# SwiGLU after polysketch attention on one core: value products of three batches as three one-pass products

## The chip, the core and the metric

The kernel runs on one core of a Trainium2 chip. The metric is the device time of one execution in microseconds, the median over several runs. Engines are named as in the profile: PE is TensorE (matrix products), PEld its weight loads, DVE is VectorE, ACT is ScalarE, POOL is GpSimd, SP is the engine that issues most DMAs.

## What is computed

Two stages follow each other. The first is attention with a polynomial sketch: for every token x of q and k two small projections a = S1 x and b = S2 x are formed (8 numbers each), and their outer product is the feature vector phi(x) (64 numbers). Then

```
kv  = sum over s of phi(k_s) v_s^T          z = sum over s of phi(k_s)
out = (phi(q) kv) / (phi(q) z + 1e-6)
```

for 4 batches, 4 heads, 1088 tokens and 32 numbers per head. The heads side by side make a matrix x of 4352 tokens by 128. The second stage is a SwiGLU block with d_ff = 1536:

```
g   = x @ w_gate
val = x @ w_val
y   = (silu(g) * val) @ w_out
```

Inputs and the output are fp32 (the kernel also takes 64-bit floats and narrows them on the chip).

## The kernel before

**Tiles.** x is kept transposed in SBUF as `xT` (128 by 4352). The tokens of a batch are cut into three blocks of 384, 384 and 320, so there are 12 blocks. d_ff is cut into 12 chunks of 128. A `unit(i, j)` (L765) is block i and chunk j: one product with `wg` into a PSUM bank `g`, one with `wv` into a bank `u`, SiLU of g on ScalarE into `sg` (L779), and on VectorE the gate product sg * u into a slot of `hbuf` (L790). `down()` (L798) multiplies the slot by `wo` and accumulates a block's 12 chunks in the bank `acc`; after the last one, `store` (L829) turns the block on VectorE (L833) and sends it out. There are 144 units, each with three fp32 products.

**Order.** The schedule is written out by hand: each engine runs its instructions in the order in which the program emits them, and waits where an operand or a buffer is not there. In batch 0 the attention comes first, then units in a hand-made list `seq` (30 units, after six early ones), with the narrowing of the weights in between. From number z = 17 of that list on a down product follows each unit; when the list ends, the remaining down products of batch 0 are drained three at a time. Then comes a loop over batches 1 to 3 and z = 0 to 35 (L1034). Each turn emits one unit, the down product that is due (`LAG = 2`: two units stay open), and one piece of the attention of later batches.

**Attention in pieces.** `attentions()` (L532) is a generator. `parts_of(n)` advances it by n pieces, most of which are one VectorE instruction; in batch 1, at z = 0, 4, 6, 7 and 8, two pieces are emitted. `group()` runs it to the next place where small TensorE products are due. There are three such places: the head of the second block of batch 1 (z = 12), the head of batch 2, and the head of its third block. A group emits `numerators` (L720), which uses the double banks `a` and `b` and writes x of a later stretch into `xT`, then, but for the last one, `values` (L634), which needs the sums of key features, and at the first group the sketches of the next batch.

**Sums.** `feature_sums` (L490) adds the key features of a batch on GpSimd in four instructions (L494), the first over 1024 columns. `key_features` (L324) and L679 are VectorE products with both inputs in SBUF, L686 is a reduction and L710 a transpose.

**PSUM.** Eight banks are given out by name: `g0`, `g1`, `g2` and `acc` singly, `a` and `b` in pairs. Units take turns over the single ones: over all four in batch 0, and over `g0` to `g2` once down products use `acc`:

```python
    free_banks = ["g0", "g1", "g2", "acc"]
    turn = [0]

    def bank(tag=None):
        if tag is None:
            tag = free_banks[turn[0] % len(free_banks)]
            turn[0] += 1
        return psum.tile([P, TB], FP32, tag=tag, name="bank")
```

Of the kernel before, what the change touches and what calls it, by code (L numbers as in the profile page):

```python
# [6 lines left out]

FP32 = mybir.dt.float32
I32 = mybir.dt.int32
U32 = mybir.dt.uint32  # L10
I64 = mybir.dt.int64
# [7 lines left out]
def kernel(  # L19
# [64 lines left out]
    free_banks = ["g0", "g1", "g2", "acc"]  # L84
    turn = [0]

    def bank(tag=None):
        if tag is None:
            tag = free_banks[turn[0] % len(free_banks)]
            turn[0] += 1  # L90
        return psum.tile([P, TB], FP32, tag=tag, name="bank")

    def wide(tag):
        return psum.tile([P, 2, TB], FP32, tag=tag, name=tag)

    nc.scalar.preload_act_table(AF.Silu)

# [359 lines left out]
    def divide(b, x0, n, nd, among=()):  # L457
# [29 lines left out]
        for name in among[1:]:  # L487
            part(name, 0)

    def feature_sums(phk):  # L490

        rows = phk[:].rearrange("p c h i j -> p c (h i j)")
        s = apool.tile([P, 4, H * F], FP32, tag="zs", name="zs")
        add = lambda o, a, b: nc.gpsimd.tensor_tensor(out=o, in0=a, in1=b, op=ALU.add)  # L494
# [37 lines left out]
    def attentions():  # L532

        yield from turns(1)
        kp, qp = wide("a"), wide("b")
        for ps, products in ((kp, key_products), (qp, query_sketches)):
            for i, c in enumerate(kpieces):
                products(ps[:, i, :], *c)
        ka = apool.tile([P, NC * H, R], FP32, tag="kas", name="kas")
        qab = apool.tile([P, 2, NC * H, R], FP32, tag="qab", name="qab", bufs=2)
        fac = None, qab

        def sketch(ps, i):  # L550
            c0, c1 = kpieces[i]
            return ps[:, i, 0 : 64 * (c1 - c0)].rearrange("p (x t r) -> p x t r", t=2, r=R)

        for i, (c0, c1) in enumerate(kpieces):
            nc.scalar.copy(ka[:, H * c0 : H * c1, :], sketch(kp, i)[:, :, 0, :])
        phk = apool.tile([P, NC, H, R, R], FP32, tag="phk", name="phk")
        for n, (i, c0, c1) in enumerate(((0, 0, 3), (0, 3, 5), (1, 5, 7), (1, 7, 9))):
            first = H * (c0 - kpieces[i][0])
            kb = sketch(kp, i)[:, first : first + H * (c1 - c0), 1, :]
            key_features(phk, (ka[:, H * c0 : H * c1, :], kb), c0, c1)  # L560
            if n < 2:
                q0, q1 = kpieces[n]
                nc.scalar.copy(
                    qab[:, :, H * q0 : H * q1, :], sketch(qp, n).rearrange("p x t r -> p t x r")
                )
            if n % 3 != 1:
                yield
        zs = feature_sums(phk)
        for i, _ in enumerate(turns(2)):
            if i % 2:  # L570
                yield
        kvz = wide("a")
        values(kvz[:, 0, :], phk, zs)
        kq = wide("b")
        fac2, copies = sketches([
            (0, NC - 1, kq[:, 0], kq[:, 1]),
            (NC - 1, NC, kvz[:, 1, 0 : 2 * F], kvz[:, 1, 2 * F : 4 * F]),
        ])
        spread = spread_out(1, kvz[:, 0, :])
        for _ in range(4):  # L580
            yield
            run_copies(copies, 1)
        step = query_step(1, fac, spread)
# [10 lines left out]
        numerators(1, spread, 3, NC)  # L594
        kv = bank()
# [6 lines left out]
        run_copies(copies, 2)  # L602
        yield
# [158 lines left out]

    lates = []

    def unit(i, j, late=False, between=(None, None)):  # L765


        t0, n = blocks[i]
        g, u = bank(), bank()
        for o, w in ((g, wg), (u, wv)):  # L770
            if between[0] and w is wv:
                between[0]()
            nc.tensor.matmul(  # L773
                o[:, 0:n], w[:, j, :], xT[:, t0 : t0 + n], start=True, stop=True
            )
# [3 lines left out]
        nc.scalar.activation(sg[:, 0:n], g[:, 0:n], AF.Silu)  # L779
        slot_of[i, j] = slots.pop(0)  # L780
        hj = hbuf[:, slot_of[i, j], :]
        hidden[i, j] = hj
        todo.append((i, j))
        if late:
            if between[1]:
                between[1]()
            nc.scalar.copy(hj[:, 0:n], u[:, 0:n])
            lates.append((hj[:, 0:n], sg[:, 0:n]))
        else:
            nc.vector.tensor_tensor(  # L790
                out=hj[:, 0:n], in0=sg[:, 0:n], in1=u[:, 0:n], op=ALU.mult
            )
# [5 lines left out]
    def down():  # L798

        i, j = todo.pop(0)  # L800
        n = SPLIT if i == LAST else blocks[i][1]
        if j == 0:
            acc[i] = bank("g1" if i == 1 else "acc")
        nc.tensor.matmul(  # L804
            acc[i][:, 0:n],
            wo[:, j, :],
            hidden[i, j][:, 0:n],
            start=(j == 0),
            stop=(j == NCH - 1),
        )  # L810
        if i != LAST:
            hidden.pop((i, j))
            slots.append(slot_of[i, j])
        if j == NCH - 1:
            store(i, n)

    def straight(ps, j):

# [180 lines left out]
    seq += [(i, j) for i in (1, 2) for j in range(3, 6)]  # L999
    seq += [(i, j) for j0 in (6, 9) for i in range(3) for j in range(j0, j0 + 3)]  # L1000
    order = [(i, j) for i in range(3) for j in range(NCH)]
    for z, (i, j) in enumerate(seq):
        if z == 17:
            free_banks.pop()
            turn[0] %= 4
        unit(i, j)
        for p in parts.get(z, ()):
            part(*p)
        if z in (24, 25, 26):
            catch_up()  # L1010
        if z == 6:
            load_k(1)
            load_v(1, [nc.sync] * 4)
            load_q(1)
# [30 lines left out]
    for j in range(NCH):  # L1045
        if todo and j % 4 == 0:
# [40 lines left out]
```

## Time and profile before

| | |
|---|---|
| time, median of 3 (range) | 305.88 us (305.69 to 307.71) |
| span of the profiled execution | 304.3 us |
| TensorE busy, share of the span | 298.0 us, 98% |
| TensorE weight loads | 190.3 us, 63% |
| VectorE | 170.0 us, 56% |
| ScalarE | 93.8 us, 31% |
| GpSimd | 37.9 us, 12% |
| mean granted TensorE clock | 0.998 |

How to read it: a line of a profile names the engine, the line of the kernel, and what it writes and reads; `xN` is the number of records. Weight loads run beside products. Ends of matmuls are modelled, so the step from one start to the next tells more than a record's length. The batch-0 list with its down products runs until about 92.5 us, the loop over batches 1 to 3 from there to about 298 us. The three groups begin at 114.6, 163.1 and 212.2 us.

### The profile page before, as it was taken

The page shows a single profiled execution, that of the slowest core. Times are in us where ns is not written, and L with a number is a line of the kernel's source. Part 1 is how long each engine was busy: PE and PEld are TensorE (multiplying, and loading weights), DVE is VectorE, ACT ScalarE, POOL GpSimd, SP SyncE. Part 2 cuts the span into 40 slices and gives each one's busy share as a digit, 9 for nine tenths or more (in the row PEclk, how much of TensorE's full clock was granted, in tenths as well). Part 3 has the DMA queues.
Part 4 walks back from the last instruction along what each step waited for, and adds up shares of the span by engine and source line. Part 5 has one row for each costly group of instructions (what it writes and reads, how often), then busy time and mean ns, then how long its engine had stood idle before and what let it go on. Part 6 is the DMA issues. An engine that isn't in the chain of part 4 may idle for free.

```text
span 304.3 us, 5402 instructions
## 1 busy us (share of the span) xinstructions
PE 298.0 (98%) x2179; PEld 190.3 (63%) x2179; DVE 170.0 (56%) x334; ACT 93.8 (31%) x219; POOL 37.9 (12%) x54
## 2 busy tenths in 40 slices
PE   8899999999999999999999999999999999999995
PEld 7545566657565556556666655555676556676664
DVE  3997988692536991788932478822423322333321
ACT  3566764422102222322222222222322222222230
POOL 3216222174000050070000000000000000000000
PEclk9999999999999999999999999999999999999999
DMA  7563490404511000400100200100100100100101
GB/s 195 150 193 106 119 302 7 149 15 149 113 28 22 0 2 22 108 0 0 26 3 2 49 0 0 28 0 0 23 5 0 22 1 2 26 0 2 21 0 26
DMA packets 26136, 14.57 MB, mean 48 GB/s; under 512 B 18688, under 2 KB 24192, under 8 KB 26112
## 3 DMA queue, kind: packets, MB, share of 16 engines
q1 hardware_dynamic: 25456, 14.13, 18.5%
q8 instruction: 17, 0.28, 0.4%
q10 hardware_dynamic: 656, 0.10, 0.2%
q14 instruction: 7, 0.06, 0.1%
HBM read 11.41 MB, written 2.23 MB: 45 GB/s over the span
## 4 chain that ended last, share of the span: by engine, by line
PE 97%; DVE 1%; issue 0%; ACT 0%
PE bank L773 58%; PE bank L804 28%; PE bank L194 2%; PE a L730 1%; PE b L289 1%; PE bank L335 1%; PE a L819 1%; PE a L301 1%; PE bank L348 0%; PE bank L301 0%; PE a L392 0%; PE a L444 0%; PE a L335 0%; PE b L301 0%; PE b L730 0%
## 5 line engine op out<-in xcount | busy, mean ns | idle before, releaser
L790 DVE TENSOR_TENSOR hbuf<-sg,bank 128x384 f32<-128x384 f32 (+1 forms) x138 | 72.9, 529 | 99.5 <-PE bank L773 97.7
L779 ACT ACTIVATE sg<-bank 128x384 f32<-128x384 f32 (+1 forms) x144 | 68.0, 473 | 163.1 <-PE bank L773 159.9
L773 PE MATMUL bank<-xT,wg 128*128 128x384 f32 (+1 forms) x288 | 112.5, 472 | 0.0
L773 PE MATMUL bank<-xT,wv 128*128 128x384 f32 (+1 forms) x288 | 111.5, 469 | 0.2 <-DVE wv L239 0.2
L804 PE MATMUL bank<-hbuf,wo 128*128 128x384 f32 (+2 forms) x288 | 105.1, 460 | 0.0
L773 PEld LDWEIGHTS bank<-xT,wv 128*128 128x128 f32 x288 | 54.5, 190 | 33.7 <-DVE hbuf L790 0.9
L804 PEld LDWEIGHTS bank<-hbuf,wo 128*128 128x128 f32 x288 | 54.6, 190 | 32.0
L773 PEld LDWEIGHTS bank<-xT,wg 128*128 128x128 f32 x288 | 53.7, 190 | 32.2 <-issue 1.6
L494 POOL TENSOR_TENSOR zs<-hbuf 128x1024 f32<-128x1024 f32 x2 | 4.7, 2359 | 51.6 <-DVE hbuf L324 37.6
L833 DVE STREAM_TRANSPOSE o<-bank 128x384 f32<-128x384 f32 (+2 forms) x12 | 6.6, 549 | 7.8 <-PE bank L804 7.4
L679 DVE TENSOR_TENSOR phq<-spread,qab 128x768 f32<-128x768 f32 x9 | 9.7, 1075 | 0.5 <-DMA spread<-spread 0.5
L221 ACT ACTIVATE exp<-exp,rebias 128x384 int32<-128x384 int32 (+3 forms) x15 | 8.3, 551 | 2.4 <-DVE exp L216 1.7
L710 DVE STREAM_TRANSPOSE phT<-phq 128x768 f32<-128x768 f32 x9 | 8.7, 968 | 0.1
L686 DVE TENSOR_REDUCE dot<-phq 128x96 f32<-128x768 f32 x9 | 8.5, 947 | 0.1
L324 DVE TENSOR_TENSOR phq<-qab 128x768 f32<-128x768 f32 x9 | 8.5, 942 | 0.0
L747 ACT COPY xT<-a 128x64 f32<-128x64 f32 (+3 forms) x7 | 2.3, 367 | 18.2 <-PE b L730 11.8
L224 DVE SCALAR_TENSOR_TENSOR exp<-raw,exp 128x384 int32<-128x384 int32 (+2 forms) x14 | 7.0, 503 | 0.0
L230 DVE SCALAR_TENSOR_TENSOR man<-raw,man 128x384 f32<-128x384 uint32 (+2 forms) x14 | 6.9, 493 | 0.0
L222 ACT ACTIVATE man<-man 128x384 f32<-128x384 int32 (+3 forms) x15 | 6.8, 452 | 0.0
L494 POOL TENSOR_TENSOR zs<-zs 128x512 f32<-128x512 f32 (+1 forms) x6 | 6.6, 1101 | 0.5
L239 POOL TENSOR_TENSOR wg<-man,exp 128x384 f32<-128x384 f32 (+1 forms) x5 | 4.0, 805 | 18.2 <-DVE man L230 14.0
L274 DVE STREAM_TRANSPOSE kT<-kld 128x384 f32<-128x384 f32 (+2 forms) x9 | 5.9, 688 | 0.3 <-DMA kld<-in_k_dram 0.3
(127 smaller groups left out, 161.4 us busy)
## 6 DMA issues: line engine op xcount, KB each, us to landing
kld<-in_k_dram SPq DMA_DIRECT2D x4, 544.0 KB, 4.3
vld<-in_v_dram SPq DMA_DIRECT2D x12, 144.0 KB, 5.1
qld<-in_q_dram SPq DMA_DIRECT2D x3, 544.0 KB, 4.2
raw<-in_moe_w_out_dram SPq DMA_DIRECT2D x4, 384.0 KB, 4.9
out_dram<-o SPq DMA_DIRECT2D x28, 48.0 KB, 1.9
raw<-in_moe_w_gate_dram SPq DMA_DIRECT2D x3, 384.0 KB, 3.6
raw<-in_moe_w_val_dram SPq DMA_DIRECT2D x3, 384.0 KB, 3.3
out_dram<-o SPq DMA_DIRECT2D x16, 40.0 KB, 1.7
```

Of the source, the lines that this page charges most:

```text
L221: nc.scalar.activation(e[:], e[:], AF.Relu, bias=rebias[: shape[0], :], scale=8.0)
L224: nc.vector.scalar_tensor_tensor(out=e[:], in0=hi, scalar=-(1 << 31), in1=e[:], op0=ALU.bitwise_and, op1=ALU.bitwise_or,)
L230: nc.vector.scalar_tensor_tensor(out=f, in0=lo, scalar=2.0**-52, in1=f, op0=ALU.mult, op1=ALU.add)
L324: engine.tensor_tensor(out=phk[:, c0:c1, :, :, :].rearrange("p c h i j -> p (c h) i j"), in0=ka.unsqueeze(3).to_broadcast([P, n, R, R]), i ...
L494: add = lambda o, a, b: nc.gpsimd.tensor_tensor(out=o, in0=a, in1=b, op=ALU.add)
L679: nc.vector.tensor_tensor(out=phq[:, c0:c1, :, :, :], in0=zrep.unsqueeze(1).to_broadcast([P, n, H, R, R]), in1=f.unsqueeze(3).to_broadcast ...
L686: nc.vector.tensor_reduce(out=dot[:, x, :], in_=phq[:, c0:c1, :, :, :].rearrange("p c h j i -> p (c h) j i"), axis=AX.X, op=ALU.add,)
L710: nc.vector.transpose(out=phT[:, :, :, c0:c1, :].rearrange("p h g c t -> p c (h g) t"), in_=phq[:, c0:c1, :, :, :].rearrange("p c h (g i) ...
L773: nc.tensor.matmul(o[:, 0:n], w[:, j, :], xT[:, t0 : t0 + n], start=True, stop=True)
L779: nc.scalar.activation(sg[:, 0:n], g[:, 0:n], AF.Silu)
L790: nc.vector.tensor_tensor(out=hj[:, 0:n], in0=sg[:, 0:n], in1=u[:, 0:n], op=ALU.mult)
L804: nc.tensor.matmul(acc[i][:, 0:n], wo[:, j, :], hidden[i, j][:, 0:n], start=(j == 0), stop=(j == NCH - 1),)
```

## The change

The value products of batches 1 to 3 are computed otherwise. An fp32 number is cut into a high part of about 12 bits and the rest, each stored as float32r[...]. With w = w1 + w0 and x = x1 + x0, and B = 4096, the program forms

```
d = (w1 - B w0) @ (x1 - B x0)
p = w1 @ x1 + (B w0) @ x0
val = (1 + 1/B) p - d / B
```

which is Karatsuba's way to the four products of parts: three one-pass products in place of one fp32 product. The purpose is to give TensorE less work. The pieces are:

- `cut_weights(c)`: for each third of four chunks, high part on ScalarE, rest on GpSimd, B times the rest on ScalarE, difference on GpSimd; 16 instructions of 384 columns in all, from z = 23 to 29 of the batch-0 list.
- `cut_tokens(i)`: for a block, high part x1 on ScalarE, rest x0 on GpSimd, difference xd on VectorE; for most blocks it is emitted at chunk 6 of the block before.
- `cut_unit(i, j)`: three one-pass products into two banks `d` and `p`, the gate product as before into `g`; u = -d/B on ScalarE, (1 + 1/B) p + u on VectorE, and the gate product with SiLU on GpSimd. After `feature_sums` the next four cut units have their gate product on VectorE (`aside=False`), while GpSimd adds the features.
- The first two units of the blocks that follow the first two groups, and the very last unit, stay `unit`.
- PSUM is one tile of eight banks. From z = 17 of the batch-0 list on, a unit gets the bank that was given out longest ago, among all that are not held; `acc` is held, `g1` while it accumulates block 1, and `a` and `b` while attention holds them. `numerators` takes `a` and `b` without holding them.

The core of the diff:

```diff
+    PS = psum.tile([P, 8, TB], FP32, name="PS")
+    place = dict(g0=0, g1=1, g2=2, acc=3, a=4, b=6)
...
     def bank(tag=None):
-        if tag is None:
-            tag = free_banks[turn[0] % len(free_banks)]
+        if tag is not None:
+            i = place[tag]
+        elif oldest[0]:
+            i = min((i for i in used if i not in held), key=used.get)
+        else:
+            i = place[free_banks[turn[0] % len(free_banks)]]
             turn[0] += 1
-        return psum.tile([P, TB], FP32, tag=tag, name="bank")
+        touch(i)
+        return PS[:, i, :]
...
     def feature_sums(phk):
+        summing[0] = 4
...
+    def cut_weights(c):
+        w = wv[:, 3 * c : 3 * c + 3, :]
...
+        nc.scalar.activation(w1[:], w, AF.Copy, scale=CUT)
+        yield
+        nc.gpsimd.tensor_tensor(out=low[:], in0=w, in1=whole(w1[:]), op=ALU.subtract)
+        yield
+        nc.scalar.activation(wb[:], low[:], AF.Copy, scale=BETA)
+        yield
+        nc.gpsimd.tensor_tensor(
+            out=wd[:], in0=whole(w1[:]), in1=whole(wb[:]), op=ALU.subtract
+        )
+        yield
+
+    def cut_tokens(i):
...
+        nc.scalar.activation(x1[:, 0:n], x, AF.Copy, scale=CUT)
+        nc.gpsimd.tensor_tensor(
+            out=x0[:, 0:n], in0=x, in1=whole(x1[:, 0:n]), op=ALU.subtract
+        )
+        nc.vector.scalar_tensor_tensor(
+            out=xd[:, 0:n], in0=whole(x0[:, 0:n]), scalar=-BETA, in1=whole(x1[:, 0:n]),
+            op0=ALU.mult, op1=ALU.add,
+        )
+
+    def cut_unit(i, j, aside=True):
...
+        d, g, p = bank(), bank(), bank()
+        nc.tensor.matmul(d[:, 0:n], wd, xd[:, 0:n], start=True, stop=True)
+        nc.tensor.matmul(
+            g[:, 0:n], wg[:, j, :], xT[:, t0 : t0 + n], start=True, stop=True
+        )
+        nc.tensor.matmul(p[:, 0:n], w1, x1[:, 0:n], start=True, stop=False)
+        nc.tensor.matmul(p[:, 0:n], wb, x0[:, 0:n], start=False, stop=True)
...
+        nc.scalar.activation(u[:, 0:n], d[:, 0:n], AF.Copy, scale=-1.0 / BETA)
...
+        nc.scalar.activation(sg[:, 0:n], g[:, 0:n], AF.Silu)
+        nc.vector.scalar_tensor_tensor(
+            out=u[:, 0:n], in0=p[:, 0:n], scalar=1.0 + 1.0 / BETA, in1=u[:, 0:n],
+            op0=ALU.mult, op1=ALU.add,
+        )
...
+        engine = nc.gpsimd if aside else nc.vector
+        engine.tensor_tensor(out=hj[:, 0:n], in0=sg[:, 0:n], in1=u[:, 0:n], op=ALU.mult)
...
     for z, (i, j) in enumerate(seq):
+        if z >= 23:
+            for c in range(max(0, z - 26), min(z - 22, len(cuts))):
+                next(cuts[c], None)
         if z == 17:
-            free_banks.pop()
-            turn[0] %= 4
+            oldest[0] = True
+            hold("acc")
...
-    for b in range(1, B):
-        for z in range(3 * NCH):
-            i, j = z // NCH, z % NCH
+    line = [3 * b + k for b in range(1, B) for k in ((0, 2, 1) if b == B - 1 else range(3))]
+    cut_tokens(line[0])
+    for at, i in enumerate(line):
+        b = i // 3
+        for j in range(NCH):
+            z = NCH * (at % 3) + j
             if (b, z) in ((1, NCH), (2, 0), (2, 2 * NCH)):
                 group()
-            unit(3 * b + ((0, 2, 1)[i] if b == B - 1 else i), j)
+                if i not in x_parts:
+                    cut_tokens(i)
+            early = (b, z // NCH) in ((1, 1), (2, 0)) and j < 2
+            last = at == len(line) - 1 and j == NCH - 1
+            if early or last:
+                unit(i, j)
+            else:
+                busy = summing[0] > 0
+                summing[0] -= 1
+                cut_unit(i, j, aside=not busy)
...
+            if j == 6 and at + 1 < len(line) and at not in (0, 2):
+                cut_tokens(line[at + 1])
```

More of the change, by code (lines that the diff above doesn't have):

```diff
@@ L8 @@
 FP32 = mybir.dt.float32
+F32R = mybir.dt.float32r
 I32 = mybir.dt.int32
@@ L85, with touch, hold, release @@
     turn = [0]
-    def bank(tag=None):
-        if tag is None:
-            tag = free_banks[turn[0] % len(free_banks)]
+    PS = psum.tile([P, 8, TB], FP32, name="PS")
+    place = dict(g0=0, g1=1, g2=2, acc=3, a=4, b=6)
+    used = {i: 0 for i in range(8)}
+    held = set()
+    oldest = [False]
+    clock = [0]
+    def touch(*which):
+        for i in which:
+            clock[0] += 1
+            used[i] = clock[0]
+    def hold(*tags):
+        for t in tags:
+            held.update((place[t], place[t] + 1) if t in "ab" else (place[t],))
+    def release(*tags):
+        for t in tags:
+            held.difference_update((place[t], place[t] + 1) if t in "ab" else (place[t],))
+    def bank(tag=None):
+        if tag is not None:
[4 more added lines that the diff above has]
+            i = place[free_banks[turn[0] % len(free_banks)]]
             turn[0] += 1
-        return psum.tile([P, TB], FP32, tag=tag, name="bank")
+        touch(i)
+        return PS[:, i, :]
     def wide(tag):
-        return psum.tile([P, 2, TB], FP32, tag=tag, name=tag)
+        i = place[tag]
+        touch(i, i + 1)
+        return PS[:, i : i + 2, :]
     nc.scalar.preload_act_table(AF.Silu)
@@ L488, in divide @@
             part(name, 0)
+    summing = [0]
     def feature_sums(phk):
+        summing[0] = 4
         rows = phk[:].rearrange("p c h i j -> p c (h i j)")
@@ L541, in attentions @@
         yield from turns(1)
+        hold("a", "b")
         kp, qp = wide("a"), wide("b")
@@ L565, in attentions @@
                 )
+            if n == 1:
+                release("b")
+            if n == 3:
+                release("a")
             if n % 3 != 1:
@@ L571, in attentions @@
                 yield
+        hold("a", "b")
         kvz = wide("a")
@@ L582, in attentions @@
             run_copies(copies, 1)
+        release("a", "b")
         step = query_step(1, fac, spread)
@@ L594, in attentions @@
         numerators(1, spread, 3, NC)
+        hold("a", "b")
         kv = bank()
@@ L602, in attentions @@
         run_copies(copies, 2)
+        release("a", "b")
         yield
@@ L763, with whole @@
     lates = []
+    BETA = 4096.0
+    CUT = 1.0 - 2.0**-13
+    val_parts = []
+    x_parts = {}
+    def whole(ap):
+        return ap.bitcast(FP32)
+    def cut_weights(c):
+        w = wv[:, 3 * c : 3 * c + 3, :]
+        w1, wb, wd = (
+            stage.tile([P, 3, P], F32R, tag=tag, name=name, bufs=6)
+            for tag, name in (("exp", "w1"), ("man", "wb"), (("exp", "man")[c % 2], "wd"))
+        )
+        low = fpool.tile([P, 3, P], FP32, tag="sgl", name="low", bufs=6)
+        val_parts.append((w1, wb, wd))
+        nc.scalar.activation(w1[:], w, AF.Copy, scale=CUT)
[8 more added lines that the diff above has]
+        yield
@@ new lines, in cut_tokens @@
+    def cut_tokens(i):
+        t0, n = blocks[i]
+        x = xT[:, t0 : t0 + n]
+        x1, x0, xd = x_parts[i] = [
+            apool.tile([P, BW], F32R, tag=tag, name=name, bufs=2)
+            for tag, name in (("qb", "x1"), ("dT", "x0"), ("rd", "xd"))
+        ]
+        nc.scalar.activation(x1[:, 0:n], x, AF.Copy, scale=CUT)
[6 more added lines that the diff above has]
+        )
@@ new lines, in cut_unit @@
+    def cut_unit(i, j, aside=True):
+        t0, n = blocks[i]
+        x1, x0, xd = x_parts[i]
+        w1, wb, wd = (w[:, j % 3, :] for w in val_parts[j // 3])
+        d, g, p = bank(), bank(), bank()
[5 more added lines that the diff above has]
+        nc.tensor.matmul(p[:, 0:n], wb, x0[:, 0:n], start=False, stop=True)
+        u = fpool.tile([P, BW], FP32, tag="sgl", name="u", bufs=6)
+        nc.scalar.activation(u[:, 0:n], d[:, 0:n], AF.Copy, scale=-1.0 / BETA)
+        sg = fpool.tile([P, BW], FP32, tag="sg", name="sg", bufs=3)
+        nc.scalar.activation(sg[:, 0:n], g[:, 0:n], AF.Silu)
+        nc.vector.scalar_tensor_tensor(
+            out=u[:, 0:n], in0=p[:, 0:n], scalar=1.0 + 1.0 / BETA, in1=u[:, 0:n],
+            op0=ALU.mult, op1=ALU.add,
+        )
+        slot_of[i, j] = slots.pop(0)
+        hj = hbuf[:, slot_of[i, j], :]
+        hidden[i, j] = hj
+        todo.append((i, j))
+        engine = nc.gpsimd if aside else nc.vector
+        engine.tensor_tensor(out=hj[:, 0:n], in0=sg[:, 0:n], in1=u[:, 0:n], op=ALU.mult)
@@ L803, in down @@
             acc[i] = bank("g1" if i == 1 else "acc")
+            if i == 1:
+                hold("g1")
         nc.tensor.matmul(
@@ L815, in down @@
             store(i, n)
+            if i == 1:
+                release("g1")
     def straight(ps, j):
@@ L1001 @@
     order = [(i, j) for i in range(3) for j in range(NCH)]
+    cuts = [cut_weights(c) for c in range(NCH // 3)]
     for z, (i, j) in enumerate(seq):
+        if z >= 23:
+            for c in range(max(0, z - 26), min(z - 22, len(cuts))):
+                next(cuts[c], None)
         if z == 17:
-            free_banks.pop()
-            turn[0] %= 4
+            oldest[0] = True
+            hold("acc")
         unit(i, j)
```

## The prediction, made before the changed kernel was run

> **What bounds the kernel now.** I read the chain of waits first, then the costliest groups, the timeline of TensorE and a table of stretches, last the timelines of VectorE and GpSimd where the change leans on them. From the page, the chain by engine and line and the five large groups:
>
> ```profile
> PE 97%; DVE 1%; issue 0%; ACT 0%
> PE bank L773 58%; PE bank L804 28%; PE bank L194 2%; PE a L730 1%; PE b L289 1%; PE bank L335 1%; PE a L819 1%; PE a L301 1%; PE bank L348 0%; PE bank L301 0%; PE a L392 0%; PE a L444 0%; PE a L335 0%; PE b L301 0%; PE b L730 0%
> ...
> L790 DVE TENSOR_TENSOR hbuf<-sg,bank 128x384 f32<-128x384 f32 (+1 forms) x138 | 72.9, 529 | 99.5 <-PE bank L773 97.7
> L779 ACT ACTIVATE sg<-bank 128x384 f32<-128x384 f32 (+1 forms) x144 | 68.0, 473 | 163.1 <-PE bank L773 159.9
> L773 PE MATMUL bank<-xT,wg 128*128 128x384 f32 (+1 forms) x288 | 112.5, 472 | 0.0
> L773 PE MATMUL bank<-xT,wv 128*128 128x384 f32 (+1 forms) x288 | 111.5, 469 | 0.2 <-DVE wv L239 0.2
> L804 PE MATMUL bank<-hbuf,wo 128*128 128x384 f32 (+2 forms) x288 | 105.1, 460 | 0.0
> ```
>
> TensorE's order is the time: it is 97% of the chain, and the other engines wait for it. 144 units leave 288 records for each product, so one fp32 product is two records. Its true price is the step from product to product in TensorE's timeline (start, duration), here in batch 1 and at the very end:
>
> ```profile
> 122.09 0.81 PE L773 MATMUL bank<-xT,wg 128*128 128x384 f32 x2
> 122.74 0.81 PE L773 MATMUL bank<-xT,wv 128*128 128x384 f32 x2
> 123.38 0.81 PE L804 MATMUL bank<-hbuf,wo 128*128 128x384 f32 x2
> ```
>
> ```profile
> 298.45 1.97 PEld L819 LDWEIGHTS a<-wo,hbuf 128*128 128x128 f32 x16
> 298.67 1.95 PE L819 MATMUL a<-wo,hbuf 128*128 128x128 f32 x16
> ```
>
> A product of 384 columns takes 0.645 us, one of 320 takes 0.54 us (150.05 to 150.59 in the same timeline), a unit of three products 1.935 us. The second fence shows that weight loads can follow each other every 1.97/16 = 0.123 us.
>
> Two stretches differ in how loaded the other engines are (busy us of PE, PEld, DVE, ACT, POOL):
>
> ```profile
> 92.50:116.50 24.00, 24.00 (x185) 14.13 (x187) 20.67 (x35) 6.43 (x14) 5.10 (x4) 1.00 0.05 8
> ...
> 200.00:300.00 100.00, 100.00 (x415) 65.54 (x414) 32.08 (x61) 25.92 (x56) 0.00 (x0) 1.00 0.05 8
> ```
>
> From 200 us on VectorE works a third of the time. In the first block of batch 1 it works 20.67 of 24 us, and its timeline has no gap from its first gate product to the last feature product of batch 2, which ends at 109.30:
>
> ```profile
> 92.70 0.52 DVE L833 STREAM_TRANSPOSE o<-bank 128x320 f32<-128x320 f32 x1 [2.50 <-PE bank L804]
> 94.06 0.55 DVE L790 TENSOR_TENSOR hbuf<-sg,bank 128x384 f32<-128x384 f32 x1 [0.84 <-PE bank L773]
> ...
> 107.42 1.88 DVE L324 TENSOR_TENSOR hbuf<-kabs 128x512 f32<-128x512 f32 x3
> ```
>
> **What the Trainium skill says.** FP8 and Floating Point Precision, section TensorE Precision Notes: true fp32 is four passes through the array, and a reduced-precision read of fp32 words exists. The trace agrees on the first: 0.645 us is four times 384 columns at 2.4 GHz (0.640). TensorE: Matmul & The Clock Gate, section Back-to-back issue gap: a warm matmul issues every N/2.4 + 2.5 ns; with the 768 columns of a record's two passes that is 0.3225 us, and two records give the measured 0.645. No row of before runs a float32r product. GPSIMD Engine Reference, section 1 (Specifications): GpSimd shares its SBUF interface with VectorE, and contends with VectorE instructions that have two SBUF inputs. The trace shows that (GpSimd's sums, then VectorE's two-input product at 0.95 us and at 2.06 us):
>
> ```profile
> 109.47 2.37 POOL L494 TENSOR_TENSOR zs<-hbuf 128x1024 f32<-128x1024 f32 x1 [37.60 <-DVE hbuf L324]
> 111.92 2.08 POOL L494 TENSOR_TENSOR zs<-zs 128x512 f32<-128x512 f32 x2
> ...
> 128.82 2.35 POOL L494 TENSOR_TENSOR zs<-hbuf 128x1024 f32<-128x1024 f32 x1 [14.02 <-PE bank L773]
> 131.25 2.67 POOL L494 TENSOR_TENSOR zs<-zs 128x512 f32<-128x512 f32 x2
> ```
>
> ```profile
> 129.93 2.06 DVE L679 TENSOR_TENSOR phq<-spread,qab 128x768 f32<-128x768 f32 x1
> ...
> 133.80 0.95 DVE L679 TENSOR_TENSOR phq<-spread,qab 128x768 f32<-128x768 f32 x1
> ```
>
> L679 began inside the sum at 128.82 and ended only 0.8 us after it; the next sum then took 0.6 us longer than its like at 111.92. The two exclude each other, an instruction at a time. A product with one input in PSUM (L790) is not held.
>
> **What the change takes off TensorE.** 108 units lie in batches 1 to 3. Four early ones and the last stay fp32; of the 103 others 67 have 384 columns and 36 have 320. Each value product goes from four passes to three. A pass costs 384/2.4 + 2.5 = 0.1625 us, or 0.136 us for 320 columns, if float32r streams a column per cycle, as each of the four fp32 passes does. Loads at 0.123 us fit beneath either. Per unit 0.645 - 0.4875 = 0.157 us, and 0.540 - 0.408 = 0.13 us; 67 x 0.157 + 36 x 0.13 = **15.2 us**. The other bound, two cycles per column (one fp32 record, 0.323 us), is a rival below.
>
> **What it puts on the others, per unit.** ScalarE: u from PSUM, 0.49 us (L779's size), together 0.98 of 1.78 us. VectorE: L790 becomes the sum of u and p, also one SBUF and one PSUM input, 0.55 us (0.47 from start to start when queued). GpSimd: the gate product, 1.0 us (L796 took 1.01 us for 128x384). All fit in 1.78 us. The product is used two units later: p ends 1.13 us into its unit and the down product starts 4.7 us in; sum and gate product take 0.2 + 0.55 + 1.0 + 0.2, so 1.6 us is left for queueing. With seven rotating banks p's bank is not asked for until 5.3 us. Where VectorE is a third busy nothing shows: the gain is whole from 200 us on.
>
> **The end of batch 0.** Eight cuts on ScalarE (4 us) and eight on GpSimd (8 us) come in from 61 us. One GpSimd cut stands ahead of the sums that start at 64.61; they end at 69.95 and TensorE reads them at 70.02, so a cut of 1.0 us less the 0.3 us of idle time there costs 0.7 us. The other cuts come behind the sums and are done by about 80, 12 us before their use. **+0.7 us.**
>
> **The first block of batch 1.** Its token cut xd stands on VectorE behind the transpose L833, which waits for the last down product: 92.70 + 0.52, then 0.5, so d starts at 93.8 instead of 92.5, and p's sum at 95.1 instead of 94.06: 1.05 us late. The first four units have their gate product on VectorE, since the counter was set in batch 0: 4 x 0.47 = 1.9 us in a queue without gaps. For the next five it is GpSimd's, against six two-input feature products; one exclusion of 1.0 us is my value, between none and three. So the features end at 109.30 + 1.05 + 1.9 + 1.0 = 113.25. GpSimd then has one more gate product ahead of its sums (0.47 + 0.1 + 1.0 = 1.55), the sums (5.34, from 109.47 to 114.81), and three VectorE gate products that shut it out (3 x 0.47 = 1.4). The sums are ready at 121.5 and TensorE needs them at the head of the second block, where it read them at 116.81. The block ends **4.7 us later** than before instead of 1.9 earlier.
>
> **The rest.** 91 units, 55 and 36: 55 x 0.157 + 36 x 0.13 = **-13.4 us**. Against it: sums beside VectorE's gate products at about 129, lagging some 2.6 us where 1.6 to 2.2 are free, 0.8; seven token cuts, where VectorE waits for two GpSimd instructions (2.0 us), mostly within the slack, 0.5; two later groups whose numerators find banks a and b lent to units, 0.4 each for one read of PSUM; the same at the last products, 0.3. Together **+2.4 us**, between 0.5 and 8.
>
> PSUM as one tile costs nothing if dependences follow regions, as hbuf's 27 slots in one tile show. Sum: 0.7 + 4.7 - 13.4 + 2.4 = -5.6, so **300.3 us**.
>
> **The rivals.** *The queues absorb it:* exclusion is rare, the sums come in time, and what is lost is the start (1.3) and 1.5 more: 305.9 - 15.2 + 2.8 = 293.5. For it: VectorE's backlog is in one block only. Against: there it has no gap to give. *VectorE and GpSimd become the bound through all attention work:* of the some 45 units between 116 and 200 us, 26 meet a two-input product, and each loses 0.45 us net instead of the 2.4 in all: 300.3 - 2.4 + 11.7 = 309.6, slower. For it: 0.47 + 0.95 + up to 1.0 exceeds 1.78 us. Against: reductions and transposes alternate with two-input products. *float32r takes two cycles per column:* 67 x 0.324 + 36 x 0.27 = +31 us, 337, slower. For it: an fp32 record is 0.323 us for two passes and could be reading its words once. Against: nothing shows it to be needed.
>
> **How the numbers follow.** Forecast 0.55, absorbed 0.27, attention-bound 0.13, two cycles 0.05. Below 302.8 lie 0.47 of the forecast and all of absorbed: faster 0.74. Within 1%: 0.08 of the forecast and 0.05 of attention-bound, 0.13. Slower 0.13. The range, 292 to 306, spans the absorbed case and the forecast with later stalls at their upper end; the two-cycle case and part of the attention-bound one stay outside.
>
> **What would show it.** Float32r records near 0.16 us apart; units after 200 us every 1.78 us (1.935 before) without TensorE idle; TensorE waiting 1.3 us for xd before the first cut unit, and several us for gate products or GpSimd's sums before the second block of batch 1; two-input VectorE products of about 2 us beside GpSimd. I am wrong if records come 0.32 us apart, if TensorE runs through the first block without waits, or if a bank of PSUM ends its waits.

## The result, and the profile after

The changed kernel takes 310.17 us (309.69 to 310.62), against 305.78 us: the ratio is 1.013, with a 95% interval of 1.0095 to 1.0163. It is slower by 1.3%, and outside the predicted range of 292 to 306 us. (305.78 is the median of four runs of the kernel before; the table further up has that of three, 305.88.)

The chain of waits of the changed kernel, from its page, and the groups that answer to those shown of before (in it L893 and L910 are the plain unit's products and gate product, L864, L868 and L869 the one-pass products, L874 the sum of u and p, L883 the gate product of a cut unit, L926 the down product):

```profile
PE 70%; DVE 13%; POOL 9%; issue 3%; DMA 1%; ACT 1%; SPq 0%; DVEq 0%; POOLq 0%; ACTq 0%
...
L883 POOL TENSOR_TENSOR hbuf<-sg,u 128x384 f32<-128x384 f32 (+1 forms) x91 | 93.3, 1030 | 88.5 <-DVE u L874 69.8
L926 PE MATMUL PS<-hbuf,wo 128*128 128x384 f32 (+2 forms) x288 | 106.9, 466 | 8.0 <-POOL hbuf L883 4.3
L874 DVE SCALAR_TENSOR_TENSOR u<-PS,u 128x384 f32<-128x384 f32 (+1 forms) x103 | 54.3, 529 | 61.4 <-PE PS L869 35.0
```

TensorE was 97% of the chain and is now 70%; VectorE and GpSimd have 22% between them. The down products, which never waited, now have TensorE stand idle for 8.0 us, 4.3 of it for gate products on GpSimd. TensorE has less to do (292.0 us busy instead of 298.0), but the span is 4.6 us longer (308.9 instead of 304.3).

Where the time went is read best by cutting both traces at the same small TensorE products: the first sketches of batch 1, and the numerators that begin each group. They start at 56.78, 88.82, 114.60, 163.07 and 212.24 us in the kernel before, and at 57.24, 91.81, 122.78, 174.46 and 221.56 us in the changed one. Since the first loads land at slightly different times, each row is the time from the row before it, in us:

| stretch | before | changed | difference | worked out in the prediction |
|---|---|---|---|---|
| sketches to first numerators (end of batch 0) | 32.04 | 34.57 | +2.5 | +0.7 |
| to the first group (block 1 of batch 1, with the last down products of batch 0) | 25.78 | 30.97 | +5.2 | +4.7 |
| to the second group (blocks 2 and 3 of batch 1) | 48.47 | 51.68 | +3.2 | about -2 |
| to the third group (two blocks of batch 2) | 49.17 | 47.10 | -2.1 | about -3 |
| to the end | 92.06 | 87.34 | -4.7 | about -6 |

(The last column's last three rows share the -13.4 us by their units, 3.1, 3.5 and 6.7, and the +2.4 of later waits: about 1.2, 0.6 and 0.6. The +4.7 was worked out for the reading of the sums, 2.2 us behind the first numerators of the group.) The first block of batch 1 loses nearly what was foretold. The other stretches fall short of it, each for its own reason. The busy times of those stretches in the changed kernel (PE, PEld, DVE, ACT, POOL):

```profile
95.70:122.80 27.10, 22.57 (x81) 14.15 (x81) 24.77 (x38) 11.79 (x24) 10.05 (x7) 1.00 0.04 7
122.80:174.50 51.70, 47.50 (x422) 33.48 (x423) 38.43 (x61) 24.25 (x55) 26.59 (x25) 1.00 0.11 24
174.50:221.60 47.10, 46.92 (x317) 32.52 (x318) 28.70 (x49) 24.70 (x52) 28.19 (x25) 1.00 0.07 13
221.60:300.00 78.40, 78.14 (x394) 58.97 (x394) 27.98 (x55) 45.17 (x99) 46.32 (x50) 1.00 0.07 10
```

TensorE has gaps in the first two and next to none in the last two. VectorE works 24.77 of 27.1 us in the first. In the second it works 38.43 of 51.7 us and GpSimd 26.59, where the kernel before has 29.98 and 6.49 in 48.5 us. VectorE's timeline of the changed kernel in the first stretch shows the steps of the prediction one by one:

```profile
95.70 0.52 DVE L957 STREAM_TRANSPOSE o<-PS 128x320 f32<-128x320 f32 x1 [2.44 <-PE PS L926]
96.14 0.52 DVE L853 SCALAR_TENSOR_TENSOR xd<-x,x 128x384 fp32r<-128x384 f32 x1
98.25 0.56 DVE L874 SCALAR_TENSOR_TENSOR u<-PS,u 128x384 f32<-128x384 f32 x1 [1.60 <-PE PS L869]
98.91 0.56 DVE L883 TENSOR_TENSOR hbuf<-sg,u 128x384 f32<-128x384 f32 x1
...
114.85 2.69 DVE L353 TENSOR_TENSOR hbuf<-kabs 128x512 f32<-128x512 f32 x3
...
119.90 1.99 DVE L883 TENSOR_TENSOR hbuf<-sg,u 128x384 f32<-128x384 f32 x1
```

The cut xd does stand behind the store's transpose (TensorE waits 1.05 us for it, where I had 1.3), the three feature products take 2.69 us where they took 1.88, and a gate product beside GpSimd's sums takes 1.99 us instead of 0.56. A gate product right behind the sum of u and p that it reads starts 0.66 us after it (98.25, 98.91), where a queued instruction follows after 0.47.

### The profile page after: what moved, and what is told of

Read it like the earlier page. It is cut to its first block, busy times and chain, and to the rows that moved or that the text cites. A ratio compares the mean times of both kernels' runs of the same rounds, so it can differ in the third digit from the quotient of the medians.

```text
span 308.9 us, 6072 instructions
## 1 busy us (share of the span) xinstructions
PE 292.0 (95%) x2282; PEld 201.2 (65%) x2282; DVE 185.3 (60%) x355; ACT 149.3 (48%) x339; POOL 147.3 (48%) x162
## 4 chain that ended last, share of the span: by engine, by line
PE 70%; DVE 13%; POOL 9%; issue 3%; DMA 1%; ACT 1%; SPq 0%; DVEq 0%; POOLq 0%; ACTq 0%
PE PS L926 22%; PE PS L865 16%; PE PS L893 12%; PE PS L864 4%; PE PS L869 4%; PE PS L868 4%; POOL zs L527 3%; DVE u L874 3%; POOL hbuf L883 2%; PE PS L772 2%; DMA kld<-in_k_dram 1%; PE PS L330 1%; DVE hbuf L353 1%; POOL low L832 1%; DVE hbuf L883 1%
## 5 line engine op out<-in xcount | busy, mean ns | idle before, releaser
L883 POOL TENSOR_TENSOR hbuf<-sg,u 128x384 f32<-128x384 f32 (+1 forms) x91 | 93.3, 1030 | 88.5 <-DVE u L874 69.8
L926 PE MATMUL PS<-hbuf,wo 128*128 128x384 f32 (+2 forms) x288 | 106.9, 466 | 8.0 <-POOL hbuf L883 4.3
L874 DVE SCALAR_TENSOR_TENSOR u<-PS,u 128x384 f32<-128x384 f32 (+1 forms) x103 | 54.3, 529 | 61.4 <-PE PS L869 35.0
L871 ACT ACTIVATE u<-PS 128x384 f32<-128x384 f32 (+1 forms) x103 | 48.7, 473 | 67.7 <-PE PS L864 67.5
L865 PE MATMUL PS<-xT,wg 128*128 128x384 f32 (+1 forms) x206 | 79.3, 467 | 0.0
L926 PEld LDWEIGHTS PS<-hbuf,wo 128*128 128x128 f32 x288 | 50.6, 188 | 22.5 <-POOL hbuf L883 7.1
L868 PE MATMUL PS<-x,w 128*128 128x384 f32 (+1 forms) x103 | 61.9, 601 | 0.0
L864 PE MATMUL PS<-xd,wd 128*128 128x384 f32 (+1 forms) x103 | 60.4, 586 | 1.0 <-DVE xd L853 1.0
L873 ACT ACTIVATE sg<-PS 128x384 f32<-128x384 f32 (+1 forms) x103 | 48.7, 472 | 19.2 <-PE PS L865 18.4
L865 PEld LDWEIGHTS PS<-xT,wg 128*128 128x128 f32 x206 | 36.4, 189 | 10.5
L869 PE MATMUL PS<-x,wb 128*128 128x384 f32 (+1 forms) x103 | 33.8, 328 | 0.0
L893 PE MATMUL PS<-xT,wv 128*128 128x384 f32 (+1 forms) x82 | 32.2, 475 | 1.3 <-DVE phk L353 0.7
L893 PE MATMUL PS<-xT,wg 128*128 128x384 f32 (+1 forms) x82 | 32.8, 482 | 0.0
L899 ACT ACTIVATE sg<-PS 128x384 f32<-128x384 f32 (+1 forms) x41 | 19.3, 474 | 21.6 <-PE PS L893 19.2
L910 DVE TENSOR_TENSOR hbuf<-sg,PS 128x384 f32<-128x384 f32 (+1 forms) x35 | 18.4, 528 | 18.0 <-PE PS L893 10.2
L864 PEld LDWEIGHTS PS<-xd,wd 128*128 128x128 f32 x103 | 19.5, 189 | 12.5 <-DVE xd L853 1.6
L869 PEld LDWEIGHTS PS<-x,wb 128*128 128x128 f32 x103 | 19.6, 190 | 11.7
L868 PEld LDWEIGHTS PS<-x,w 128*128 128x128 f32 x103 | 19.5, 190 | 11.8
L893 PEld LDWEIGHTS PS<-xT,wv 128*128 128x128 f32 x82 | 15.2, 190 | 12.0 <-ACT sg L899 1.5
L893 PEld LDWEIGHTS PS<-xT,wg 128*128 128x128 f32 x82 | 14.7, 189 | 10.1 <-issue 1.2
L853 DVE SCALAR_TENSOR_TENSOR xd<-x,x 128x384 fp32r<-128x384 f32 (+1 forms) x9 | 4.8, 531 | 13.6 <-POOL x L850 13.6
```

The costliest lines, as they stand in the source:

```text
L864: nc.tensor.matmul(d[:, 0:n], wd, xd[:, 0:n], start=True, stop=True)
L865: nc.tensor.matmul(g[:, 0:n], wg[:, j, :], xT[:, t0 : t0 + n], start=True, stop=True)
L868: nc.tensor.matmul(p[:, 0:n], w1, x1[:, 0:n], start=True, stop=False)
L869: nc.tensor.matmul(p[:, 0:n], wb, x0[:, 0:n], start=False, stop=True)
L871: nc.scalar.activation(u[:, 0:n], d[:, 0:n], AF.Copy, scale=-1.0 / BETA)
L874: nc.vector.scalar_tensor_tensor(out=u[:, 0:n], in0=p[:, 0:n], scalar=1.0 + 1.0 / BETA, in1=u[:, 0:n], op0=ALU.mult, op1=ALU.add,)
```

## Experiments

The theory after the result: the passes saved are real but smaller than worked out; the bank order costs time of its own; and in batch 1 VectorE and GpSimd together get more work than fits beside attention. The rivals: exclusion of VectorE and GpSimd alone; gate products that come too late for the two open units; the weight cuts. A further one came out of the traces only afterwards and is not tested: the place of a token cut in the order (see the edit e9_gate_psum).

### The bank order alone (e1_psum)

```diff
-        if z >= 23:
-            for c in range(max(0, z - 26), min(z - 22, len(cuts))):
-                next(cuts[c], None)
...
-    cut_tokens(line[0])
...
-                if i not in x_parts:
-                    cut_tokens(i)
...
-            if early or last:
+            if True:
                 unit(i, j)
```

> Only the new order of PSUM banks: every unit of batches 1 to 3 is a plain one, no weights or tokens are cut. Theory of the prediction (one PSUM tile and the longest-unused rule cost nothing): 305.8 +-0.5. Rival, from the changed kernel's trace, where TensorE waited 0.7 us at 64 us for a bank that the attention was still reading: 306.5 to 307.5, with the same wait at the same place. If the bank order were the whole loss at the end of batch 0 (3.0 us), 308 to 309.

Measured: 308.37 us against 306.09, ratio 1.0068 (1.0042 to 1.0095). (The run with the trace is the longest of seven, 309.91 us; its first sketches start at 58.59 us, 1.8 later than before, which the stretches leave out.) The end of batch 0 takes 33.91 us instead of 32.04; all other stretches lie within 0.15 us of before. So **the bank order alone costs about 2 us**, nearly all of it in one place, and the expectation that it costs nothing (305.8) is refuted. Two waits in TensorE's timeline of this kernel:

```profile
66.40 0.91 PE L893 MATMUL PS<-xT,wv 128*128 128x384 f32 x2 [0.69 <-DVE phk L353]
80.79 11.78 PE L926 MATMUL PS<-hbuf,wo 128*128 128x384 f32 x38 [0.65 <-DVE hbuf L910]
```

In the first, `release` gives bank pair `a` back when the last feature product has been emitted; by then it is the pair used longest ago, so the very next unit gets it, and its product waits until VectorE has run that feature product (L353). In the second, the accumulation of block 1 claims `g1`, which the rule has just lent to the last unit, and waits for that unit's gate product. "Given out longest ago" counts the order of the program, not the moment at which the reader will be done.

### The order of the products in a unit (e2_order)

```diff
         nc.tensor.matmul(d[:, 0:n], wd, xd[:, 0:n], start=True, stop=True)
+        nc.tensor.matmul(p[:, 0:n], w1, x1[:, 0:n], start=True, stop=False)
+        nc.tensor.matmul(p[:, 0:n], wb, x0[:, 0:n], start=False, stop=True)
         nc.tensor.matmul(g[:, 0:n], wg[:, j, :], xT[:, t0 : t0 + n], ...)
-        nc.tensor.matmul(p[:, 0:n], w1, x1[:, 0:n], start=True, stop=False)
-        nc.tensor.matmul(p[:, 0:n], wb, x0[:, 0:n], start=False, stop=True)
```

> The changed kernel with its three one-pass products next to each other (d, p, p, then the gate product). In the changed kernel a cut unit of 384 columns takes 1.815 us in the quiet stretch where 1.78 was expected. If the 0.035 us come at each change between fp32 and float32r products, half of these changes go and the unit takes 1.80, the whole 308 to 309. If they belong to each one-pass product (0.175 us instead of 0.1625), the unit stays at 1.815 and the time at 310.

Measured: 309.71 us, 0.46 below the changed kernel's, whose runs overlap its own; the last stretch takes 87.14 us instead of 87.34. The unit stays at 1.82 us. TensorE's timeline with the new order, where L865 and L866 are the two products into p and L867 is the gate's:

```profile
251.16 0.63 PE L864 MATMUL PS<-xd,wd 128*128 128x384 f32 x1
251.63 0.34 PE L865 MATMUL PS<-x,w 128*128 128x384 f32 x1
251.81 0.34 PE L866 MATMUL PS<-x,wb 128*128 128x384 f32 x1
251.99 0.81 PE L867 MATMUL PS<-xT,wg 128*128 128x384 f32 x2
252.63 0.81 PE L926 MATMUL PS<-hbuf,wo 128*128 128x384 f32 x2
252.98 0.63 PE L864 MATMUL PS<-xd,wd 128*128 128x384 f32 x1
```

Next to each other, the two products into p start 0.18 us apart. With half of the changes between kinds gone, the unit would take 1.80 us if the extra came with them; it does not, so as far as these two orders show the extra belongs to the pass. From the unit times: (1.815 - 1.29)/3 = 0.175 us for 384 columns and (1.515 - 1.08)/3 = 0.145 for 320, that is 0.455 us per 1000 columns, where an fp32 pass takes about 0.42.

### All gate products on VectorE, or all on GpSimd (e3_gate_vector, e4_gate_gpsimd)

```diff
-                cut_unit(i, j, aside=not busy)
+                cut_unit(i, j, aside=False)
```

In e4 it is `aside=True`.

> The changed kernel with every gate product of a cut unit on VectorE, none on GpSimd. Theory that VectorE's own work is the bound in the attention stretches: it gains some 40 products of 0.47 us there, less what it no longer waits for GpSimd (1 to 2 us per block): 313 to 318. Rival, that the loss is mainly the exclusion of VectorE and GpSimd: the two-input products return to 0.95 us, and the time falls to 305 to 309. From 222 us on (VectorE 28 of 78 us busy) no difference either way.

> The changed kernel with every gate product of a cut unit on GpSimd, also while it adds the features. Theory that VectorE is the bound in batch 1: the first block gets 1.9 us shorter at its start, but three gate products queue behind 5.3 us of sums and TensorE waits for them at two places, 2 to 4 us each: 309 to 314. Rival, that VectorE's gate products held up inside the sums (2.8 us where one takes 0.56) are the main loss: 304 to 308.

Measured: 319.48 us and 314.5 us, both a little beyond the worse case. On VectorE alone, block 1 of batch 1 takes 33.30 us (30.97 in the changed kernel) and the next two 55.03 (51.68), of which VectorE is busy 45.0; even the two blocks of batch 2 rise from 47.10 to 50.57, and the last stretch, where I expected no difference, from 87.34 to 87.98. On GpSimd alone the first two are 32.81 and 53.55. Either way is worse, so the changed kernel's split is better than its ends. Taking GpSimd's gate products away did not bring the time down: for e3 the rival, exclusion as the main loss, is refuted, and so is e4's. Both edits also add work to one engine, so they do not tell what the exclusion costs in the changed kernel.

### Gate products that are not shut out by the sums (e9_gate_psum)

```diff
+        if not aside:
+            sg = g
         nc.scalar.activation(sg[:, 0:n], g[:, 0:n], AF.Silu)
```

> The changed kernel, but where a gate product is VectorE's, ScalarE writes SiLU into the gate's own PSUM bank, so that VectorE's product has one input in SBUF and one in PSUM. Theory that the exclusion of two-input VectorE products and GpSimd's sums holds these products up (2.0 and 2.8 us for 0.56): each takes 0.55 us again, and the blocks of batch 1 end 2 to 4 us earlier: 306 to 308. Rival, that the sums wait just as long elsewhere: 309 to 310.

Measured: 310.46 us, no change against 310.17. The edit did what it should, as VectorE's timeline of this kernel shows (L885 is its gate product, L853 makes xd of the next block):

```profile
141.09 0.56 DVE L885 TENSOR_TENSOR hbuf<-PS,u 128x384 f32<-128x384 f32 x1
143.08 0.56 DVE L885 TENSOR_TENSOR hbuf<-PS,u 128x384 f32<-128x384 f32 x1
143.56 2.05 DVE L721 TENSOR_TENSOR phq<-spread,qab 128x768 f32<-128x768 f32 x1
147.85 0.49 DVE L853 SCALAR_TENSOR_TENSOR xd<-x,x 128x320 fp32r<-128x320 f32 x1 [2.25 <-POOL x L850]
```

The gate products are back at 0.56 us, but the next product with two inputs in SBUF now takes 2.05 us beside the sums (0.95 alone, 1.48 in the changed kernel), and then VectorE stands idle for 2.25 us: xd needs GpSimd's part of the token cut, and that stands behind the sums. Block 1 gains 0.4 us and the next two lose 0.9. My expectation of 2 to 4 us is refuted; the wait moved to other instructions. The edit also has a side effect: the gate's bank is not free until VectorE has run the gate product, and TensorE's longest wait in these blocks is now for such a bank (2.30 us at 149.53).

The same token cut stands before the longest wait of TensorE in blocks 2 and 3 of the changed kernel (from the timelines of GpSimd, VectorE and TensorE):

```profile
145.26 0.92 POOL L527 TENSOR_TENSOR zs<-zs,hbuf 128x256 f32<-128x256 f32 x1
146.14 1.59 POOL L850 TENSOR_TENSOR x<-xT,x 128x320 fp32r<-128x320 f32 x1
147.76 0.49 DVE L853 SCALAR_TENSOR_TENSOR xd<-x,x 128x320 fp32r<-128x320 f32 x1 [0.77 <-POOL x L850]
148.83 0.56 DVE L883 TENSOR_TENSOR hbuf<-sg,u 128x384 f32<-128x384 f32 x1
149.44 0.91 PE L926 MATMUL PS<-hbuf,wo 128*128 128x384 f32 x2 [1.71 <-DVE hbuf L883]
```

As far as the traces show, part of that loss hangs on the place of one token cut in the order of GpSimd and VectorE. No run moves it, so what another place would gain is not shown.

### Four open units (e5_lag4)

```diff
-    LAG = 2
+    LAG = 4
```

This kernel leaves out the last down product of the last block and the store that follows it, some 0.4 us of TensorE.

> The changed kernel with four open units instead of two before a down product, so that a gate product has 3.6 us more to arrive. If TensorE's waits for gate products in the first two blocks of batch 1 are a matter of latency, they go (about 7 us of them outside the groups) and the time is 303 to 306. If VectorE and GpSimd together have more work there than TensorE, the waits only move to the next group: 308.5 to 310.5.

Measured: 309.92 us. Block 1 of batch 1 takes 28.28 us instead of 30.97, of which 1.29 are two down products that now come later, and blocks 2 and 3 take 53.85 instead of 51.68. TensorE's waits for gate products are gone in batch 1, and others stand in their place (from its timeline):

```profile
108.19 0.44 PE L864 MATMUL PS<-xd,wd 128*128 128x384 f32 x1 [0.65 <-DVE u L874]
...
122.76 1.23 PE L772 MATMUL PS<-phT,spread 32*32 32x192 f32 x62 [2.55 <-DVE u L874]
...
148.67 0.45 PE L864 MATMUL PS<-xd,wd 128*128 128x384 f32 x1 [1.66 <-DVE u L874]
```

Now it is a PSUM bank that VectorE has not read. More room between the engines brings nothing on the whole, so the theory that gate products merely come too late for two open units falls. It does not follow that all of it is VectorE's load: before the last of these waits VectorE had stood idle for 2.24 us, until 147.65, for the token cut behind GpSimd's sums.

### Four gate products less on VectorE (e10_first_four)

```diff
     cut_tokens(line[0])
+    summing[0] = 0
     for at, i in enumerate(line):
```

> The changed kernel with the counter of GpSimd's sums put back to 0 before batch 1, so that the first four gate products of its first block go to GpSimd, which is idle there. Theory that VectorE's queue without gaps sets the end of the block: 1.9 us of VectorE work go, less some 0.5 us of exclusion against its two-input products; the first group starts 1 to 2 us earlier and the time is 308.3 to 309.5. If something else holds the block, the time stays at 310.

Measured: 307.48 us, 2.7 us below the changed kernel, and 1.0051 (1.0034 to 1.0067) of before. Block 1 falls from 30.97 to 28.62 us, and every later stretch is as it was to 0.02 us. The gain is more than the 1 to 2 us that I expected. Each of the four gate products stands right behind the sum that it reads, so it takes 0.66 us of VectorE's queue and not the 0.47 charged, 2.6 in all; the block is 2.35 us shorter. So **there VectorE's queue is the time**, at nearly the full price; the difference leaves some 0.3 us for the exclusion that GpSimd's products bring back in exchange, less than the 0.5 I had allowed.

### Block 1 plain, batch 1 plain (e11_block3_plain, e6_batch1_plain)

```diff
-    cut_tokens(line[0])
...
-            if early or last:
+            if early or last or at == 0:
                 unit(i, j)
+                summing[0] -= at == 0
```

In e6 the condition is `early or last or i < 6`, and tokens are cut from block 6 on.

> The changed kernel with plain units in the first block of batch 1 alone; everything after it as changed. From the traces that block costs 5.2 us more than before, the next two 3.2 more, and both together give 8.4. If the losses stand apart, the time falls by 5 to 304.5 to 305.5 and the stretch from the first to the second group stays at 51.7 us (48.5 before). If the second loss came from the first (a late queue handed on), that stretch falls below 49 and the time to 302.

> The changed kernel with plain units in batch 1; cut units begin with batch 2. Measured unit times (1.815 for 1.935, 1.515 for 1.615) give 45 x 0.12 + 24 x 0.10 = 7.8 us off. The bank order costs 2.1 (the kernel with that alone), the weight cuts at the end of batch 0 0.7, waits in the attention of batch 3 about 1. Theory that the whole of batch 1's cut units is a loss: 305.9 - 7.8 + 3.8 = 302. Rival, that the waits of batch 1 come with any cut unit beside attention: 304 to 306, with waits of several us before the head of the third block of batch 2.

Measured: 304.36 us, ratio 0.9956 (0.9941 to 0.997), and 302.65 us, ratio 0.9897 (0.9882 to 0.9911). With block 1 plain its stretch is 25.71 us, as before; the next is 50.70, between the 51.7 and the 49 of my two cases, so of its loss of 3.2 us 1.0 was handed on from block 1 and 2.2 is its own. With batch 1 plain that stretch is 48.46. From batch 2 on e6 gains 6.2 us on the kernel before, and e11 6.9, whatever stands ahead. So the losses stand apart for the most part, as the first theory had it, and blocks 2 and 3, beside the queries of batch 2 and the keys of batch 3, are a loss by themselves.

### Late cuts (e7_late_cuts)

```diff
-            oldest[0] = True
+            free_banks.pop()
+            turn[0] %= 4
             hold("acc")
...
+            if (b, z) == (2, 0):
+                oldest[0] = True
+                summing[0] = 0
+            if b == 1 and z >= 24:
+                for c in range(max(0, z - 27), min(z - 23, len(cuts))):
+                    next(cuts[c], None)
```

(Against the changed kernel, with e6's plain batch 1 and without the weight cuts in batch 0.)

> As the kernel with plain units in batch 1, and besides the old turn of banks until batch 2 begins, and the weight cuts on ScalarE and GpSimd in the third block of batch 1, where GpSimd is idle. If bank order and weight cuts are what is lost at the end of batch 0, 2.8 us come back: 299 to 300, with the first numerators 32.0 us after the first sketches as in the kernel before (34.6 in the changed one). If the loss there has another cause, 301 to 302.

Measured: **298.69 us**, ratio 0.9769 (0.9755 to 0.9784): faster than both kernels, and slightly below the expected 299 to 300. The gain on the kernel before is 7.1 us of the 7.8 that its cut units allow (45 x 0.12 + 24 x 0.10). The end of batch 0 takes 32.03 us again, so bank order and weight cuts were what was lost there. From its page, the busy times and the chain by engine:

```profile
PE 290.4 (98%) x2248; PEld 197.7 (67%) x2248; DVE 172.9 (58%) x340; ACT 132.0 (44%) x302; POOL 122.0 (41%) x137
...
PE 93%; DVE 2%; DMA 1%; POOL 1%; issue 1%; ACT 0%; SPq 0%; POOLq 0%; DVEq 0%
```

TensorE is busy 98% of the span, as before the change, but of a shorter span, and VectorE and GpSimd have 3% of the chain where they had 22%.

### The third block of batch 1 as well (e12_with_block5)

Against the kernel with late cuts (e7):

```diff
-            if (b, z) == (2, 0):
+            if (b, z) == (1, 24):
...
-            if b == 1 and z >= 24:
-                for c in range(max(0, z - 27), min(z - 23, len(cuts))):
+            if b == 1 and 17 <= z <= 23:
+                for c in range(max(0, z - 20), min(z - 16, len(cuts))):
...
-            if early or last or i < 6:
+            if early or last or i < 5:
```

> The kernel with late cuts (298.7), with the third block of batch 1 also in cut units and the weight cuts in the second. VectorE works 13 of 22 us there. If only VectorE's load decides, 12 x 0.10 = 1.2 us come off: 297.3 to 298. If GpSimd's eight weight cuts, next to its sums and to two-input VectorE products, hold VectorE up: 299 to 300.

Measured: 300.9 us, 2.2 more than e7: a miss, beyond even the worse of the two cases. Blocks 2 and 3 of batch 1 take 50.36 us where e7 has 48.35. ScalarE's and TensorE's timelines show the two longest waits in them:

```profile
136.22 0.52 ACT L834 ACTIVATE wb<-low 128x384 fp32r<-128x384 f32 x1 [2.87 <-POOL low L832]
136.65 0.51 ACT L830 ACTIVATE w<-wv 128x384 fp32r<-128x384 f32 x1
137.06 0.47 ACT L899 ACTIVATE sg<-PS 128x384 f32<-128x384 f32 x1
```

```profile
137.58 0.91 PE L893 MATMUL PS<-xT,wv 128*128 128x384 f32 x2 [1.25 <-ACT sg L899]
150.24 0.78 PE L926 MATMUL PS<-hbuf,wo 128*128 128x320 f32 x2 [0.71 <-DVE o L957]
```

The second weight cut on ScalarE waits 2.87 us for a GpSimd cut that stands behind the sums. A SiLU is queued behind it on ScalarE, and TensorE waits for the bank that this SiLU should have read. The changed kernel shows the same at the end of batch 0: SiLU's bank held TensorE for 0.40 us, shortly before the drain, after ScalarE had waited 4.2, 1.5 and 1.5 us for such cuts. The second wait of e12, 0.71 us, is for the store's transpose on VectorE, which comes late; VectorE had itself waited 2.39 us for a token cut behind the sums (at 137.03).

## Why the prediction was wrong, point by point

**What bounds the kernel before: right.** TensorE's order was the time, and where the others had room (from batch 2 on) the passes saved came off the span.

**"What the change takes off TensorE", 15.2 us: the mechanism right, the size off.** One pass per product was right: 0.175 us is near the expected 0.16 and far from 0.32, so the rival of 337 us is out. But the pass was sized by the Trainium skill, TensorE: Matmul & The Clock Gate, section Back-to-back issue gap (N/2.4 + 2.5 ns: 0.1625 us, and 0.136). That section gives the formula for an isolated matmul and says that it over-counts at large N in a stream; here it under-counts, with 0.175 and 0.145 us measured, and the measurement decides. A unit gains 0.12 us or 0.10, and 67 x 0.12 + 36 x 0.10 = **11.6 us** is the whole of it. This term was 3.6 us too large. What the extra 12 ns of a pass (9 at 320 columns) are is open; e2 shows only that they do not go with the changes between fp32 and float32r.

**"PSUM as one tile costs nothing": wrong.** It was true of the tile, and I had stopped there. The rule that hands banks out costs about 2 us, by e1. I had charged lent banks only at the two later groups (0.4 each), where e1 shows less than 0.15 in each stretch, and not at the end of batch 0, where they matter. "A bank of PSUM ends its waits" was one of my own signs of being wrong, and at the end of batch 0 it came true (0.69 and 0.40 us in the changed kernel).

**"The end of batch 0", +0.7: right in size for the cuts, wrong in its way.** The changed kernel has 34.57 us there and e1 33.91, so the cuts add 0.66. But the step said that a GpSimd cut makes the sums late. TensorE reads them 14.20 us after the first sketches in both kernels, with cuts and without (13.24 before), so if they are late it is hidden behind the wait for the bank. What I left out is the ScalarE instruction that waits for GpSimd, and the SiLU queued behind it. I had named what stands ahead on GpSimd, and not what stands behind on ScalarE. e12 showed the cost of the same omission more plainly.

**"The first block of batch 1", +4.7: right in size and in VectorE's queue, not in the wait that ends last.** Measured +5.2 at the head of the group, and +5.5 where TensorE reads the sums. The steps of the queue are there: xd behind the store, no gap for four gate products on VectorE (e10: 2.35 us for the four, 1.9 charged), exclusion of GpSimd and two-input products by 1.4 us in the features (1.0 taken). The sums end at 124.83 us, 121.8 if one takes off the 3.0 us by which this kernel's block began later; 121.5 was worked out. But TensorE does not wait for the sums: it reads them at 125.33, straight behind the value products, as before. What it waits for ahead of the group, 4.6 us in all, is xd (1.05) and then gate products (0.21, 1.71, 0.26, 0.69 and 0.66), which the sum for this block left out. The sums and the gate products stand behind the same queue of VectorE; that they come out so close is in part luck. It is also here that the trace agreed with the Trainium skill's GPSIMD Engine Reference, section 1, on the shared SBUF interface: the gate product with two inputs in SBUF took 1.99 us beside the sums instead of 0.56.

**"The rest", +2.4 against 13.4: the failing step.** The three later stretches gave 3.6 us where 11.0 was worked out. 3.1 of the missing 7.4 are the pass size on 55 and 36 units. The other 4.3 lie in the second and third block of batch 1, which cost 3.2 more than before, where about 2 less was expected. There TensorE stands idle 3.4 us for gate products (0.28, 1.71, 0.41 and 1.02 us). The terms for it were 0.8 us for sums beside gate products and 0.5 for all seven token cuts, "mostly within the slack"; the wait of 1.71 us, behind one such token cut, exceeds both together. I had found for the first block that VectorE has no gap, and for these only compared single waits with the slack of one unit (1.6 us), as if each wait began with empty queues; in fact GpSimd's gate products, its sums, the token cut and VectorE's own products stand one behind the other from 138.8 to 149.4 us. e5 shows that two more open units do not bring the time back; e3 and e4 that neither engine can take the gate products whole; e11 that only 1.0 us is handed on. The rival in which attention binds, 309.6 with a chance of 0.13, was the nearest to what happened, in its number partly by luck: of the 9.9 us between 300.3 and 310.17, 3.6 are the size of a pass and 1.9 the bank order, and neither is part of it.

**What stays open:** in those two blocks, how the loss divides between VectorE's own work, the exclusion and the place of the token cut behind the sums. e9 took the exclusion from some gate products, and the time went into another product and into waiting for that cut. A kernel in which no product has two inputs in SBUF wasn't tried, nor one that emits the token cut ahead of the sums.

## What to carry to other kernels

Before moving work from the engine that bounds to others, add up the load of each of them stretch by stretch: where one of them has no gap, as VectorE in block 1 here, what is added there is the time at nearly its full price, and two more open units did not help. An instruction that waits for a slow engine also holds all that is queued behind it on its own engine, as a weight cut on ScalarE held a SiLU and a token cut on VectorE a gate product. So make such a change where the others have room: the same one-pass products from batch 2 on, with the weights cut in the block before and the new bank order only from there on, gave 298.69 us where the whole change gave 310.17.

## What the runs showed that was not expected

A one-pass float32r product takes about 0.455 us per 1000 columns (0.175 us for 384, 0.145 for 320), some 8% more than a pass of an fp32 product in the same unit (0.161 and 0.135). And with one input in PSUM a VectorE product passes beside GpSimd's sums at 0.56 us where it takes 1.99 or 2.76 us from SBUF alone, yet this freed nothing: the next two-input product took over the wait, and a token cut behind the sums the rest.
